# Attention and expert layers on one Trainium2 core: idle TensorE products moved to the first place, and the last part of q loaded by one DMA

## The chip, the cores and the metric

The kernel runs on one core of one Trainium2 chip. The metric is the device time of one execution in microseconds; several executions are made, and their median counts. A profiled execution of the kernel before gives the trace from which all rows below come.

## The reference

Two computations follow each other. The first is an attention with pooled queries, the second an expert layer over its output.

```python
q_pool = q.reshape(B, H, S // 2, 2, D).mean(axis=3)          # B 4, H 8, S 1152, D 64
scores = scale * np.matmul(q_pool, k.transpose(0, 1, 3, 2))
attn = exp(scores - max) / (sum + 1e-09)
x = np.matmul(attn, v)                                        # to 2304 tokens x 512
h = x @ w_in                                                  # 512 x 2048
g = np.where(h > 0.0, h, np.exp(np.minimum(h, 0.0)) - 1.0)
out = g @ w_out                                               # 2048 x 512
```

## The kernel before

The work of one batch item is a unit (four units); a unit has four pairs of heads, and a pair has nine attention steps: for each head four blocks of 128 pooled queries, and a last block of 64 for both heads together. A step computes scores on TensorE into the only score buffer `s` (L935 and L941 for a pair in plain float32, which the first pair is), takes their largest on VectorE into an `ep` buffer (`biggest`, L985), the exponential on ScalarE (L991), and turns the result by products with the identity (L1067) before it is multiplied with v. Since there is one buffer `s`, the scores of a step wait until L985 of the step before has read them. The expert layer of a unit (L1229, L1310) is spread between the attention steps of the next unit; the weights of both its matrices are first decoded on VectorE by three instructions each half (`dec`, L820, L821, L824), 512 KB a half.

Before the first step, `prep` fetches and turns the operands of the first pair. k comes in two DMAs on SP's queue (`load_k`, L600). q comes on ScalarE's queue: two DMAs of 256 KB, one for each head (`load_qa`, L585), and the last 128 rows of each head, 64 pooled queries, by `load_qb` (L591, with the issue at L593): a loop of two DMAs of 32 KB, each from 64 places of 512 bytes to 64 partitions. Behind them in SP's queue stand three halves of w_in (L805) and then the q of the second pair (L558, L563), which goes to the same tile and so waits until the first pair's q has been read. VectorE adds the two rows of each pooled query (`qtwice`, L655): blocks 4 to 7 first, then 0 to 3, then block 8, which is the part that `load_qb` brings. TensorE turns k and the sums (L624), ScalarE takes the results from PSUM (L627).

The order of the work on each engine is written out: `ORDER` (L32) lists task numbers with a letter for the engine (p TensorE, v VectorE, a ScalarE, g GpSimd, s the DMA queue of SP), and each engine works through its own tasks in exactly this order. `SLOTS` (L190) gives the buffer of each tile. In the list the addition of block 8 is `19v`; behind it on VectorE stand `301v` and `316v`, the decoding of the first two weight halves, and then `415v`, the first L985. ScalarE begins with `4a`, `3a` (load_qa) and `5a` (load_qb). TensorE begins with `11p` and `9p`, which turn k.

One task, `0p`, is `warm` (L758): six products of the identity with itself into a PSUM buffer that nobody reads. In the list before it stands between `20p`, the turning of block 8, and `437p`, the scores of the third step. The costs given to `plan.add` (900.0 for load_qb, 1530.0 for warm) belong to the planner that once wrote the list; the kernel as it is run reads the list only.

Of the kernel before, what the change touches and what calls it, by code (L numbers as in the profile page):

```python
# [19 lines left out]
CFG = dict(  # L20
    MODE=0,
    LOADS=-2465884, WI0=-27823, WIT=30440, WO0=1311932, WOT=4783, T0=1480, T1=812, M0=21242,
    M1=58392, KS=5164412, KM=-16195, KE=597808, KH=-20226, KL=126077, KV=-42119, KN=-15967,
    KX=-43605, KO=-36554, PEN=-18129, W0L=26355, WIN=-42633, PD=3605, KS0=29075649, KM0=3580,
    KE0=43169, KH0=-7128, KL0=17190, KV0=-37362, KX0=35076, PLM0=0, NS0=36, PLM=0, M2=6438, DP=0,
    FK=0, PENW=-13844, PENH=10146, FL=2000, PH0=2, PH=1, KT=140078, KT0=-327, LV=15492, PENN=-24464,
    PENT=-48259, PLP=1, WLP=1, HIP=1, PENM=0, L0=1000000, PA=9244, PB=93473, KA=40989, KB=-4257737, KC=34460,
    PENR=0,
# [1 line left out]


ORDER = """  # L32
2s 1s 11p 4a 16v 299s 9p 3a 314s 13v 5a 12a 10a 19v 17p 7p 283s 18a 414p 22s 288s 8a 301v 23s 316v
370s 294s 415v 14p 15a 427p 285v 20p 21a 428v 429a 0p 437p 435p 289s 431p 27p 34g 416a 31v 290v
319s 422p 438v 28a 404p 372v 32p 29p 439a 432a 423a 417g 405v 35p 25p 26a 406a 36a 291v 460p 461v
440g 441p 442a 321v 37g 42s 38p 40s 433p 30a 462a 434a 33a 450p 451v 443p 296v 418p 407g 436a 496p
497v 452a 419a 444a 293s 410p 420p 421a 45a 292a 39v 453g 458p 459v 408p 409a 6s 313s 309s 463v
# [150 lines left out]
"""  # L188

SLOTS = """  # L190
# [147 lines left out]
def attention_moe_kernel(  # L338
# [9 lines left out]
    nc = tc.nc  # L348
# [12 lines left out]
    plan = Plan()  # L361
# [40 lines left out]
    def act(n):  # L402
        return 0.95 * n + 70.0
# [4 lines left out]
    def dve(n):  # L408
        return Port(1.08 * n + 75.0)
# [4 lines left out]
    def pol(n):  # L414
        return 0.93 * n + 150.0

    def pol2(n):
        return Port(1.9 * n + 190.0)
# [18 lines left out]
    for b, s0, nt, lo in [(b, 0, 4, True) for b in range(0, B)]:  # L437
        u = Rec()
# [5 lines left out]
        while t0 < u.n:  # L444
            n = 256 if u.n - t0 != 320 else 320
# [102 lines left out]
    def prep(pr, t0, t1):  # L548
        u, p = pr.u, pr.p
        b, nq = u.b, u.nq  # L550
        q32, k32, qT, kT, v32 = (plan.buf(x) for x in ("q32", "k32", "qT", "kT", "v32"))
        pr.kT, pr.qT, pr.v32 = kT, qT, v32
        key = [t0 + (t1 - t0) * j / 16.0 for j in range(16)]
        lk = key[0] - (LOADS if pr.i else CFG["L0"])
# [27 lines left out]
        def load_qa(h):  # L582
            def load_qa():
                src, t = q[b, 2 * p + h, 2 * u.s0:], u.nt
                nc.scalar.dma_start(  # L585
                    out=q32.ap[:, t * h:t * h + t].rearrange("p t r d -> p (t r d)"),
                    in_=src[0:256 * t].rearrange("(p c) d -> p (c d)", p=128),
                )
            return load_qa

        def load_qb():  # L591
            for h in range(2):
                nc.scalar.dma_start(  # L593
                    out=q32.ap[64 * h:64 * h + 64, 2 * u.nt],
                    in_=q[b, 2 * p + h, 2 * u.s0 + 256 * u.nt:][0:128].rearrange("(p r) d -> p r d", r=2),
                )

        def load_k(h):
            def load_k():
                nc.sync.dma_start(out=k32.ap[:, h], in_=k[b, 2 * p + h].rearrange("(p c) d -> p c d", p=128))  # L600
            return load_k

        n = nq * 64
        q_s = lambda: q32.ap[:, :nq, 0]
        if pr.i == 0:
            tk = [plan.add("DMA", Move(450.0, 1100.0), lk + h, load_k(h), (), [k32], lag=LAND) for h in range(2)]
            tq = [plan.add("ACT", 450.0 + h, lk - 10.0 + h, load_qa(h), (), [q32]) for h in range(2)]
            tq.append(plan.add("ACT", 900.0, lk - 8.0, load_qb, (), [q32]))
        else:
            tq = [plan.add("DMA", Move(1700.0, 2200.0), lk - 10.0, load_q, (), [q32], lag=LAND)] * 3  # L610
        qa = None if pr.plain else plan.add("DVE", dve(n), key[0], qadd(nc.vector), [tq[0]], [q32], [("POOL", pol2(n) + 90.0, qadd(nc.gpsimd))])
# [62 lines left out]
        def hi(dst, src, j):  # L674
            def hi_act():
                nc.scalar.activation(out=dst(), in_=src(), func=AF.Copy, scale=sm.ap[:, 8 + j:9 + j])

            def hi_pool():
                ts(nc.gpsimd, dst(), src(), sm.ap[:, 8 + j:9 + j], 1.0)

            def hi_dve():
                ts(nc.vector, dst(), src(), sm.ap[:, 8 + j:9 + j], 1.0)

            hi_act.__name__ += str(j)
            return hi_act, hi_pool, hi_dve

        def lo(dst, src, h, j):
            def lo_dve():
                pairs_ = [(dst(), src(), h())]
                if len(dst().shape) == 4 and j <= 1:  # L690
                    pairs_ = [tuple(x()[:, :, a] for x in (dst, src, h)) for a in range(2)]
                for o, i, m in pairs_:
                    nc.vector.scalar_tensor_tensor(
                        out=o, in0=i, scalar=sm.ap[:, 8 + j:9 + j], in1=m, op0=ALU.mult, op1=ALU.subtract
                    )

            def lo_pool():
                ts(nc.gpsimd, src(), src(), sm.ap[:, 8 + j:9 + j], 1.0)
                nc.gpsimd.tensor_tensor(out=dst(), in0=src(), in1=h(), op=ALU.subtract)

            lo_dve.__name__ += str(j)
            return lo_dve, lo_pool

        def halves(n, kh, kl, dst_h, dst_l, src, j, after, bufs):
            f, g, d = hi(dst_h, src, j)
            h = plan.add("ACT", act(n), kh, f, after, bufs, [("POOL", pol(n), g), ("DVE", Port(0.58 * n + 90.0), d)])
            f, g = lo(dst_l, src, dst_h, j)
            t = plan.add("DVE", Port(730.0, 730.0) if j == 1 else dve(n) + 35.0 * (j == 0), kl, f, [h], bufs, [("POOL", Port(pol(n), pol2(n)), g)] if CFG["PLP"] else [])
            t.pen = CFG["PENH"]
            return t  # L710

# [19 lines left out]
        sc = summed(lambda: sm.ap[:, 0:nsum], nsum, key[3], sums, [sm], up)  # L731
        pr.sc = [sc]
        ql = halves(n, key[4], key[5], q_h, q_l, q_s, 0, [sc], [qn, q32, sm])

        def q_t():
# [14 lines left out]
        qw = plan.add("DMA", Move(1180.0, 1400.0), key[9], q_lo, [qt], [qT], lag=1000.0)  # L750
        pr.qs = lambda st: qw
        kl = halves(1152, key[6], key[7], k_h, k_l, k_s, 1, [sc, sums[-1]], [kn, k32, sm])
        pr.kdone = [[plan.add("DMA", Move(3400.0, 3000.0, True), key[9], k_t, [kl], [kn, kT], lag=1100.0)]] * 2
        pr.vdone = [halves(1152, key[11], key[12], v_h, v_l, v_s, 2, [sc], [v16, v32, sm])] if pr.split else [tv]

    idle = plan.buf("r")

    def warm():  # L758
        for i in range(6):
            nc.tensor.matmul(idle.ap[:, 0:128], ident, ident, start=True, stop=True)  # L760

    plan.add("PE", 1530.0, -1.0e9, warm, [], [idle])

    for pr in pairs:
        plan.at = str(pr.u.i)
        if pr.i == 0:
            prep(pr, -9000.0, 0.0)
        else:
            prev = pairs[pr.i - 1]
            prep(pr, prev.t0 - CFG["PA"], pr.t0 - CFG["PB"])  # L770
# [115 lines left out]
    r = plan.add("DVE", 150.0, WI0 + WIT * NG, wi_top, wi_max)  # L886
# [20 lines left out]
    r = plan.add("DVE", 150.0, 0.0, wo_top, wo_max)  # L907
# [476 lines left out]
```

## Time and profile before

| what | us |
| --- | --- |
| median of 3 executions | 742.1 (742.02 to 743.98) |
| profiled execution, its time | 742.65 |
| span of its trace, first to last instruction | 740.9 |
| TensorE busy in the span | 717.3 (97%) |
| VectorE busy | 625.0 (84%) |
| ScalarE busy | 560.6 (76%) |
| GpSimd busy | 338.0 (46%) |

The span is what the rows add up to; 1.75 us of the profiled execution lie outside it. Busy shares over the whole span hide that the engines take turns as the bound, so the rows below are of short stretches, most of them of the first 20 us, where the change is.

### The profile page before, as it was taken

Reading aid. Unit: us, or ns where it says so; the run is one execution under the profiler, and the core shown is the slowest. Engines: PE = TensorE matmul, PEld = TensorE weight load, DVE = VectorE, ACT = ScalarE, POOL = GpSimd, SP = SyncE. Lnnn points to the kernel's source line nnn. Section 1 sums busy time; section 2 is a strip of 40 time slices with the busy share of each in tenths; the row PEclk is TensorE's granted clock in tenths of the full one; section 3 lists DMA queues with packets and bytes.
Section 4 is the critical chain, followed back from the end, with each engine's and each line's share of the span. In section 5 each row is a group of like instructions: output and inputs, shape, how many; then the busy total and the mean of one; then the engine's idle time right before and its main releaser. Section 6 shows DMA issues by size and latency. Waiting matters only on the chain.

```text
span 740.9 us, 19632 instructions
## 1 busy us (share of the span) xinstructions
PE 717.3 (97%) x7905; PEld 478.8 (65%) x7905; DVE 625.0 (84%) x1098; ACT 560.6 (76%) x974; POOL 338.0 (46%) x385
## 2 busy tenths in 40 slices
PE   5899998999999999999999999999999999999997
PEld 4577776877565555775676566786665665865753
DVE  6999999999998998879898879899988989875330
ACT  3899997998998887777688766889788564752651
POOL 1322455466626633376465554354646452440430
PEclk9999999999999999999999999999999999999999
DMA  8787834577999998999999999899899998793001
GB/s 304 287 228 251 247 119 105 142 135 160 171 179 207 178 204 169 211 181 174 213 171 208 189 205 181 163 162 209 173 189 194 188 162 137 139 139 64 30 1 36
DMA packets 310971, 126.01 MB, mean 170 GB/s; under 512 B 286304, under 2 KB 288352, under 8 KB 310880
## 3 DMA queue, kind: packets, MB, share of 16 engines
q1 hardware_dynamic: 310432, 124.16, 82.4%
q8 instruction: 62, 1.02, 0.6%
q10 hardware_dynamic: 448, 0.59, 0.2%
q14 instruction: 29, 0.24, 0.1%
HBM read 45.09 MB, written 4.72 MB: 67 GB/s over the span
## 4 chain that ended last, share of the span: by engine, by line
PE 47%; DVE 3%; ACT 2%; issue 1%; DVEq 0%; ACTq 0%
PE r L1310 16%; PE r L1229 14%; PE r L1119 6%; PE s L956 4%; PE s L970 3%; PE r L1101 1%; DVE ep L985 1%; PE r L1067 1%; ACT ep L991 1%; PE s L961 0%; DVE ep L1045 0%; DVE tmp L1265 0%; DVE x L1207 0%; DVE g L1291 0%; ACT hb L1042 0%
## 5 line engine op out<-in xcount | busy, mean ns | idle before, releaser
L991 ACT ACTIVATE ep<-ep,wk 128x1152 f32<-128x1152 f32 x136 | 170.4, 1254 | 45.7 <-DVE ep L985 40.5
L1229 PE MATMUL r<-x,wi 128*128 128x256 f16 (+1 forms) x1536 | 196.6, 286 | 1.5 <-DVE tmp L1265 1.5
L985 DVE TENSOR_SCALAR_CACHE_REDUCE ep<-s,sm 128x1152 f32<-128x1152 f32 x122 | 172.3, 1412 | 13.0 <-PE s L970 9.2
L1229 PEld LDWEIGHTS <-wi 128*128 128x128 f16 x1536 | 147.6, 98 | 43.6 <-issue 6.1
L1310 PE MATMUL r<-wo,g 128*128 128x512 f16 (+1 forms) x864 | 174.9, 380 | 0.1
L1045 DVE SCALAR_TENSOR_TENSOR ep<-ep,wk,hb 128x1152 f16<-128x1152 f32 x99 | 146.0, 1478 | 6.7 <-ACT hb L1042 4.7
L1310 PEld LDWEIGHTS <-g 128*128 128x128 f16 (+1 forms) x864 | 73.3, 100 | 83.8 <-issue 4.7
L956 PE MATMUL s<-kT,qT 128*128 128x512 f16 (+3 forms) x420 | 82.9, 328 | 4.3 <-DVE ep L985 3.3
L1119 PEld LDWEIGHTS <-v 128*64 128x64 f16 x2970 | 77.8, 110 | 11.4 <-issue 10.5
L1119 PE MATMUL r<-pT,v 128*64 128x128 f16 (+1 forms) x2970 | 84.4, 215 | 0.3 <-DVE tmp L1265 0.3
L1283 POOL TENSOR_TENSOR g<-tmp,g 128x320 f16<-128x320 f32 (+1 forms) x61 | 68.1, 1118 | 36.0 <-ACT g L1279 34.4
L499 POOL TENSOR_SCALAR wk<-wk 128x1 f32<-128x1 f32 x68 | 31.2, 459 | 114.3 <-ACT ep L991 93.9
L1042 ACT ACTIVATE hb<-ep,wk 128x1152 f16<-128x1152 f32 x50 | 62.3, 1249 | 17.3 <-POOL wk L1010 8.2
L1036 POOL TENSOR_SCALAR hb<-ep,wk 128x1152 f16<-128x1152 f32 x34 | 44.3, 1303 | 56.6 <-DVE wk L1001 29.6
L1265 DVE SCALAR_TENSOR_TENSOR tmp<-r,tmp 128x320 f32<-128x320 f32 (+1 forms) x96 | 51.5, 551 | 21.5 <-POOL tmp L1250 11.5
L1242 ACT ACTIVATE tmp<-r 128x320 f32<-128x320 f32 (+1 forms) x96 | 45.1, 480 | 23.0 <-PE r L1229 14.7
L1245 ACT ACTIVATE tmp<-tmp,us 128x320 f32<-128x320 f32 (+1 forms) x96 | 57.8, 610 | 2.0 <-DVE us L1184 0.5
L956 PEld LDWEIGHTS <-qT 128*128 128x128 f16 (+1 forms) x420 | 33.9, 100 | 37.4 <-issue 13.7
L970 PE MATMUL s<-kT,qT 64*128 64x512 f16 (+1 forms) x280 | 49.6, 391 | 0.9 <-DVE ep L985 0.9
L1077 ACT ACTIVATE pT<-r 128x384 f32<-128x384 f32 x96 | 43.7, 498 | 8.7 <-PE r L1067 8.4
L1067 PE MATMUL r<-ident,ep 128*128 128x128 f32 x333 | 47.3, 283 | 2.3 <-DVE x L1134 2.3
L1287 POOL TENSOR_SCALAR g<-tmp 128x320 f16<-128x320 f32 (+1 forms) x42 | 28.8, 686 | 39.5 <-DVE tmp L1265 39.5
(163 smaller groups left out, 1044.0 us busy)
## 6 DMA issues: line engine op xcount, KB each, us to landing
v<-in_v_dram SPq DMA_DIRECT2D x16, 576.0 KB, 4.3
k<-in_k_dram SPq DMA_DIRECT2D x15, 576.0 KB, 4.5
g<-in_moe_w_in_dram SPq DMA_DIRECT2D x15, 512.0 KB, 7.2
q<-in_q_dram SPq DMA_DIRECT2D x15, 512.0 KB, 4.3
g<-in_moe_w_out_dram SPq DMA_DIRECT2D x15, 512.0 KB, 5.4
out_dram<-tmp SPq DMA_DIRECT2D x16, 256.0 KB, 3.0
qT<-qT SPq DMA_DIRECT2D x28, 144.0 KB, 3.0
pT<-hb SPq DMA_TRANSPOSE x99, 3.6
```

The source lines that it names most:

```text
L956: nc.tensor.matmul(s.ap[rows, c, 0:n], pr.qT.ap[:, 1 - c % 2, j, rows], keys[h][c], start=first[c], stop=not first[c] and c < 2, skip_grou ...
L970: nc.tensor.matmul(s.ap[rows, c, 0:512], pr.qT.ap[r, c, j, rows], keys[h][c][r], start=first[c], stop=not first[c], skip_group_check=True,)
L985: nc.vector.tensor_scalar(e_(), s.ap.rearrange("p a b -> p (a b)")[:, 0:S], -0.5 / float(D) ** 0.5 if pr.plain else pr.sm.ap[:, 12:13], No ...
L991: nc.scalar.activation(out=e_(), in_=e_(), func=AF.Exp, bias=nm.ap[:, 0:1], scale=-1.0, accum_out=nm.ap[:, 1:2],)
L1042: nc.scalar.activation(out=hb.ap, in_=e_(), func=AF.Copy, scale=nm.ap[:, 1:2])
L1045: nc.vector.scalar_tensor_tensor(out=e16(), in0=e_(), scalar=nm.ap[:, 1:2], in1=hb.ap, op0=ALU.mult, op1=ALU.subtract)
L1067: nc.tensor.transpose(tp.ap[:, c * 128:(c + 1) * 128], e_()[:, (j + c) * 128:(j + c + 1) * 128], ident)
L1119: nc.tensor.matmul(half(h), pr.v16.ap[:, h, order[c], e], p, start=(j + c == 0), stop=(j == 2 and c == NCH - 1), skip_group_check=True,)
L1229: nc.tensor.matmul(hp.ap[:, f * n:(f + 1) * n], w_in16[g][:, a, c, (f0 + f) * 128:(f0 + f + 1) * 128], x16.ap[:, e, c, g0:g0 + n], start=( ...
L1245: nc.scalar.activation(out=en.ap[:, :m], in_=en.ap[:, :m], func=AF.Exp, scale=us.ap[:, 8:9])
L1283: nc.gpsimd.tensor_tensor(out=l, in0=gv, in1=h, op=ALU.subtract)
L1310: nc.tensor.matmul(op.ap[r0:r0 + tn, :], gt[qd].ap[:, a, fi, o:o + tn], w_out16(f // 2)[:, e, f % 2, :], start=(i < 128 // tn), stop=(i >= ...
```

## The change

It makes three edits. The idle products are seven and stand first in TensorE's order. The last part of q comes by one DMA that covers both heads; its destination is 128 partitions of 512 bytes, its source two heads of 64 places of 512 bytes. Five PSUM buffers of the first part are renumbered: the idle products write buffer 0, and the turnings of k and q that used 3, 1, 2 and 0 use 4, 2, 3 and 1. The rest of `ORDER` and `SLOTS` is unchanged, and the changed costs are the planner's alone.

```diff
 ORDER = """
-2s 1s 11p 4a 16v 299s 9p 3a 314s 13v 5a 12a 10a 19v 17p 7p 283s 18a 414p 22s 288s 8a 301v 23s 316v
-370s 294s 415v 14p 15a 427p 285v 20p 21a 428v 429a 0p 437p 435p 289s 431p 27p 34g 416a 31v 290v
+0p 2s 1s 11p 4a 16v 299s 9p 3a 314s 13v 5a 12a 10a 19v 17p 7p 283s 18a 414p 22s 288s 8a 301v 23s
+316v 370s 294s 415v 14p 15a 427p 285v 20p 21a 428v 429a 437p 435p 289s 431p 27p 34g 416a 31v 290v
...
 SLOTS = """
-01 00 00 00 03 00 01 00 00 04 00 02 00 00 00 01 00 01 04 04 00 01 01 03 03 00 00 02 00 00 00 02 00
+00 00 00 00 04 00 02 01 00 00 00 03 01 00 00 01 00 01 04 04 00 01 01 03 03 00 00 02 00 00 00 02 00
...
         def load_qb():
-            for h in range(2):
-                nc.scalar.dma_start(
-                    out=q32.ap[64 * h:64 * h + 64, 2 * u.nt],
-                    in_=q[b, 2 * p + h, 2 * u.s0 + 256 * u.nt:][0:128].rearrange("(p r) d -> p r d", r=2),
-                )
+            nc.scalar.dma_start(
+                out=q32.ap[:, 2 * u.nt].rearrange("p r d -> p (r d)"),
+                in_=q[b, 2 * p:2 * p + 2, 2 * u.s0 + 256 * u.nt:][:, 0:128].rearrange("h (p r) d -> h p (r d)", r=2),
+            )
...
     def warm():
-        for i in range(6):
+        for i in range(7):
             nc.tensor.matmul(idle.ap[:, 0:128], ident, ident, start=True, stop=True)
 
-    plan.add("PE", 1530.0, -1.0e9, warm, [], [idle])
+    plan.add("PE", 1820.0, -1.0e9, warm, [], [idle])
```

## Rows read from the trace of the kernel before

**Rows 1.** Busy time by stretch: span, PE, PEld, DVE, ACT, POOL, PEclk, DMA, GB/s
```profile
core 0: us, PE busy (x) PEld busy (x) DVE busy (x) ACT busy (x) POOL busy (x), PEclk, DMA share, GB/s
...
6.00:9.00 3.00, 2.98 (x15) 2.67 (x15) 1.46 (x4) 1.47 (x3) 0.00 (x0) 1.00 1.06 384
9.00:12.00 3.00, 2.99 (x11) 1.55 (x10) 2.90 (x6) 0.60 (x1) 0.00 (x0) 1.00 0.94 269
12.00:15.00 3.00, 1.50 (x8) 0.97 (x9) 2.93 (x6) 0.60 (x1) 0.00 (x0) 1.00 0.89 280
...
60.00:90.00 30.00, 30.00 (x342) 23.18 (x342) 28.82 (x67) 28.73 (x59) 10.16 (x14) 1.00 0.86 263
...
117.00:124.00 7.00, 3.48 (x29) 2.35 (x24) 6.93 (x10) 5.18 (x11) 5.23 (x3) 0.99 0.71 190
124.00:127.30 3.30, 3.30 (x17) 2.41 (x14) 2.80 (x10) 0.58 (x2) 0.00 (x0) 0.51 0.89 187
...
300.00:600.00 300.00, 298.28 (x3529) 197.56 (x3528) 266.50 (x450) 231.83 (x394) 160.83 (x180) 1.00 1.00 188
```

**Rows 2.** Waits of VectorE, 8 to 124 us: total, times, longest
```profile
DVE kn L655 <- DMA q<-in_q_dram: 1.3, 1, 1.3
```

**Rows 3.** Timeline of VectorE, 4 to 20 us: start, duration, what, idle before
```profile
8.20 0.29 DVE L655 TENSOR_TENSOR kn<-q 128x128 f32<-128x128 f32 x1 [1.27 <-DMA q<-in_q_dram]
8.41 0.42 DVE L820 TENSOR_SCALAR tmp<-h 128x512 uint32<-128x512 uint32 x1
...
11.38 0.69 DVE L824 SCALAR_TENSOR_TENSOR wi<-g,tmp 128x512 uint32<-128x512 uint32 x1
11.99 1.35 DVE L985 TENSOR_SCALAR_CACHE_REDUCE ep<-s 128x1152 f32<-128x1152 f32 x1
...
15.06 1.35 DVE L985 TENSOR_SCALAR_CACHE_REDUCE ep<-s 128x1152 f32<-128x1152 f32 x1
```

**Rows 4.** Timeline of TensorE, 0 to 30 us
```profile
6.02 1.30 PE L624 MATMUL r<-ident,k 128*128 128x128 f32 x5 [6.02 <-DMA k<-in_k_dram]
...
8.96 2.08 PE L935 MATMUL s<-kT,qT 64*128 64x512 f32 x4
10.83 0.56 PE L941 MATMUL s<-kT,qT 64*128 64x128 f32 x2
11.33 0.66 PE L624 MATMUL r<-ident,kn 128*128 128x128 f32 x4
13.49 1.13 PE L935 MATMUL s<-kT,qT 64*128 64x512 f32 x4 [1.50 <-DVE ep L985]
14.43 0.38 PE L941 MATMUL s<-kT,qT 64*128 64x128 f32 x2
...
14.90 1.50 PE L760 MATMUL r<-ident 128*128 128x128 f32 x12
16.47 1.13 PE L935 MATMUL s<-kT,qT 64*128 64x512 f32 x4
```

**Rows 5.** Timeline of the first 30 us: GpSimd's last work on the identity, and load_qb's issues
```profile
1.00 0.29 POOL masks.py:199 TENSOR_SCALAR_AFFINE_SELECT ident<-ident 128x128 f32<-128x128 f32 x1
...
1.65 1.16 ACTq L593 DMA_DIRECT2D q<-in_q_dram  x2
```

**Rows 6.** DMA by queue, 0 to 30 us: packets, MB, share of 16 engines
```profile
q10 hardware_dynamic: 448, 0.59, 5.6%
```

**Rows 7.** DMA issues of 2.0 to 2.3 us: KB each, median us to landing
```profile
h<-in_moe_w_in_dram SPq DMA_DIRECT2D x1, 512.0 KB, 6.3
...
q<-in_q_dram ACTq DMA_DIRECT2D x2, 32.0 KB, 5.9
```

**Rows 8.** DMA issues of 1.6 to 1.7 us: the second load_qa
```profile
q<-in_q_dram ACTq DMA_DIRECT2D x1, 256.0 KB, 5.0
```

**Rows 9.** The third half of w_in: its issue in SP's timeline, 3.4 to 6 us
```profile
4.93 0.37 SPq L805 DMA_DIRECT2D g<-in_moe_w_in_dram  x1
```

**Rows 10.** DMA issues of 3.5 to 6 us: the same load's landing
```profile
g<-in_moe_w_in_dram SPq DMA_DIRECT2D x1, 512.0 KB, 5.6
```

More of the change, by code (lines that the diff above doesn't have):

```diff
@@ L607, in prep @@
             tq = [plan.add("ACT", 450.0 + h, lk - 10.0 + h, load_qa(h), (), [q32]) for h in range(2)]
-            tq.append(plan.add("ACT", 900.0, lk - 8.0, load_qb, (), [q32]))
+            tq.append(plan.add("ACT", 470.0, lk - 8.0, load_qb, (), [q32]))
         else:
@@ L707, in halves @@
             f, g = lo(dst_l, src, dst_h, j)
-            t = plan.add("DVE", Port(730.0, 730.0) if j == 1 else dve(n) + 35.0 * (j == 0), kl, f, [h], bufs, [("POOL", Port(pol(n), pol2(n)), g)] if CFG["PLP"] else [])
+            t = plan.add("DVE", Port(730.0, 730.0) if j == 1 else Port(*[0.5 * dve(n) + 17.5] * 2) if j == 0 else dve(n), kl, f, [h], bufs, [("POOL", Port(pol(n), pol2(n)), g)] if CFG["PLP"] else [])
             t.pen = CFG["PENH"]
```

## The prediction

> **What bounds the kernel now.** I read the busy time by stretch first, then who waits for whom, then the timeline of the first 20 us. In the middle, from 300 to 600 us, TensorE has no gaps worth the name: 298.28 of 300 us busy [rows 1]. But the change is made at the very start, and there another engine sets the pace. From 9 us on VectorE is busy 2.90 of every 3 us while TensorE drops to 1.50 [rows 1], and between 8 and 124 us VectorE waits for a measurable time exactly once: 1.3 us for a DMA of q [rows 2]. That wait ends at 8.20, when VectorE adds the last part of q [rows 3]; the last part is what the changed DMA brings. Behind it VectorE runs without a hole: two weight halves decoded from 8.41 to 12.07, the first L985 at 11.99, three more decoding instructions, the second L985 at 15.06 [rows 3]. At 117 to 124 us TensorE is the one that stands idle (3.48 of 7 us busy) beside a VectorE at 6.93 [rows 1]. So up to 124 us a delay of VectorE's chain at 8.20 is passed on whole, and after that TensorE's full queue passes it on too. Nothing downstream has slack to swallow it.
>
> The idle products stand at 14.90 to 16.40, and the next scores start at 16.47 [rows 4], when the second L985 has read the single buffer `s` (15.06 + 1.35 = 16.41 [rows 3]). They fill a hole; they hold up nothing.
>
> **The change, part by part.** *Six products taken from 14.9:* 12 instructions, 1.50 us [rows 4], worth nothing, since the cover is L985 and stays.
>
> *Seven put first:* they need only the identity, ready at 1.29 [rows 5]. Their price without warm-up is bounded by the same form later, 14 x 125 ns = 1.75 us, and by the slowest early turning, 1.30 us / 5 = 0.26 us each [rows 4], so 3.6 us. From 1.35 that ends at 3.1 to 5.0, ahead of 6.02, when k lands [rows 4]. Cost zero, with 1 us of cover left.
>
> What they could gain is a faster clock for TensorE's first real work. The clock column says 1.00 there, but the durations say otherwise: four score products take 2.08 us at 8.96 and 1.13 us at 13.49, and turnings go from 0.26 to 0.165 us at 11.33 [rows 4]. So up to about 11 us TensorE ran at the lower of its levels, 1.2 GHz, and then at 2.4. Yet a faster start pays almost nothing: the first scores end at 11.39 [rows 4], and L985 begins at 11.99 because VectorE is decoding until then [rows 3]. Between nothing and a few tenths; I take zero.
>
> *Buffers renumbered:* the turning that gets buffer 4 a second time stands behind the first scores in TensorE's order, and the buffer's reader is done by then. Zero.
>
> *The last part of q by one DMA.* On ScalarE's queue one issue goes (two take 1.16 us [rows 5]); ScalarE has nothing else to do then, so nothing. What counts is when the data land. Now the two DMAs start at 1.65 and 2.20 and land 5.9 us later [rows 5, 7], at 7.55 and 8.11, which is the 8.20 of VectorE.
>
> How is a DMA dealt out to the 16 engines? The queue of these four DMAs shows 448 packets [rows 6]. From the code, 256 are rows of 2 KB and 128 are places of 512 bytes; the 64 left are 16 for each DMA, one closing write per engine. So each ran on all 16. In each, both sides had 64 or 128 as their outermost length. In the new one the destination has 128, but the source has 2: the heads lie 1152 rows apart, so its two blocks cannot be read as one run. No row shows such a DMA. The ends are 16 engines and 2. Equal shares of the outermost length explain the 16 of all the old ones, and here leave only shares of two; I take 2 engines.
>
> The Trainium skill ("DMA: Bandwidth & Descriptors", section on why a DMA increments its semaphore by 16) gives this as the rule: the count is the largest up to 16 that divides the outermost lengths of both sides. By it the merged DMA runs on 2 engines, with 16 the sum would be about zero; no trace here has tested it yet.
>
> The price by rows: the 16 engines together move 384 GB/s between 6 and 9 us [rows 1], 24 GB/s each. Two engines get 32 KB each in place of 4 KB. At the least that is 28 KB more at 24 GB/s, 1.2 us: landing at 9.3. At the most, every 512-byte packet waits for a 2 KB packet of SP's queue: 64 times 2.5 KB at 24 GB/s is 6.8 us, from the landing of the second load_qa at 6.16 [rows 8] to 13.0. Between them: SP's early loads end with the third weight half, 4.93 + 5.6 = 10.5 [rows 9, 10], on these two engines 1.2 us later, 11.7; by then 52 of the 64 packets are through, and the rest take 0.3 us. I take 11.9, nearest to the upper end since the queues are full there: **3.8 us later** than 8.11.
>
> The weight half that is decoded next landed at 1.63 + 6.3 = 7.9 [rows 7], so it is not the next to be late. SP's queue is: the second pair's q waits for this tile, and all loads behind it with it; but their readers on VectorE move by the same 3.8 us.
>
> *What follows from the gap:* TensorE, done at 12.0, would wait until 13.49 + 3.8 = 17.3 for its second scores [rows 4], with one small turning in between. The one fall of the clock in these stretches came behind a hole: 3.48 of 7 us busy, then 0.51 granted [rows 1], so 1.2 GHz. Scores at half speed last 2.43 us (8.96 to 11.39) against 1.32 (13.49 to 14.81) [rows 4]: 1.1 us a step while the step is bound by this loop. I count one step, 1.1 us; none is the lower end, three (3.3 us) the upper.
>
> **The sum.** Profiled execution 742.65 + 3.8 + 1.1 = 747.5; the median lies 0.55 lower, so 742.1 + 4.9 = **747.0 us**. This case's own range: 742.1 + 1.2 = 743.3 to 742.1 + 4.9 + 3.3 = 750.3.
>
> **The rivals.** *Sixteen engines after all (not slower).* The merged DMA is one packet per engine shorter and lands between 7.55 and 8.11. VectorE then goes on until the weight half at 7.9 stops it, so it gains 0 to 0.3 us: 741.8 to 742.1. For it: every DMA in the trace used 16. Against: none had an outermost length of 2. It decides at the landing: below 8.2 it is this.
>
> *The hole at 14.9 costs the clock.* With the idle products gone and the DMA harmless, TensorE rests at 12.0 to 13.49 and again at 15.1 to 16.47. If the clock falls, one to three score steps cost 1.1 us each: 743.2 to 745.4. Against: 12 to 15 us has 1.50 of 3 us busy and the clock stays 1.00 [rows 1].
>
> *The early clock pays.* If the seven products raise the clock before 6 us and the DMA lands early, L985 starts 0.3 us sooner, 741.8, no more, by the decoding ahead of it.
>
> **How the numbers follow.** Two engines 0.60, sixteen with nothing else 0.30, the hole's clock alone 0.06, the early clock 0.04. A measurement tells 0.3%, 2.2 us: the limits are 739.9 and 744.3. Of the two-engine case about 0.08 stays under 744.3 (early landing, clock kept), 0.52 is above; of the hole 0.02 is above. That makes slower 0.54, and the rest, less 0.03 for what I have not seen, the same. The range runs from 741.0, below the sixteen-engine case by what executions scatter, to 749.3; it leaves the far end of the clock's fall out.
>
> **What would show it.** Right: block 8's addition at about 12 us, the first L985 at 15.8, slow score products near 17, and 384 + 16 + 16 + 2 = 418 packets on ScalarE's queue; 432 would mean sixteen engines. Wrong: that addition at 8.2 or sooner, with VectorE's chain where it was. If it comes at 12 and the end does not move, the claim that VectorE's chain is passed on whole was wrong.

## The result, and the profile after

The changed kernel takes 747.75 us (median of 6 executions, 745.76 to 749.44), the kernel before 742.06 us beside it: a ratio of 1.007 with a 95% interval of 1.0051 to 1.009, 5.7 us slower. The profiled execution took 749.06 us with a span of 747.3.

The first view is the timeline of VectorE in the changed kernel (start, duration, what, idle time before). Lines have moved up by one: L654 is the addition of q, L984 the first pass over the scores.

```profile
6.30 0.69 DVE L654 TENSOR_TENSOR kn<-q 128x512 f32<-128x512 f32 x1 [0.63 <-DMA q<-in_q_dram]
11.54 0.29 DVE L654 TENSOR_TENSOR kn<-q 128x128 f32<-128x128 f32 x1 [4.54 <-DMA q<-in_q_dram]
...
15.33 1.35 DVE L984 TENSOR_SCALAR_CACHE_REDUCE ep<-s 128x1152 f32<-128x1152 f32 x1
...
19.34 1.36 DVE L984 TENSOR_SCALAR_CACHE_REDUCE ep<-s 128x1152 f32<-128x1152 f32 x1 [0.86 <-PE s L940]
...
23.31 1.35 DVE L984 TENSOR_SCALAR_CACHE_REDUCE ep<-s 128x1152 f32<-128x1152 f32 x1
...
27.54 1.36 DVE L984 TENSOR_SCALAR_CACHE_REDUCE ep<-s 128x1152 f32<-128x1152 f32 x1 [1.08 <-PE s L940]
...
30.62 1.35 DVE L984 TENSOR_SCALAR_CACHE_REDUCE wo<-s 128x1152 f32<-128x1152 f32 x1
```

Block 8 is added at 11.54, where it was at 8.20 [rows 3]: VectorE stands idle for 4.54 us, waiting for the last part of q. The first L984 comes at 15.33 in place of 11.99 [rows 3], the same 3.34 us. Then a second loss joins: the next one is 4.28 us late (19.34 against 15.06 [rows 3]), and VectorE now waits for the scores, 0.86 and 1.08 us, which it never did before [rows 2]. The fifth starts at 30.62; in the kernel before it started at 24.86, so that 5.76 us are lost by then. This is the row of the kernel before, from the same view:

```profile
24.86 1.35 DVE L985 TENSOR_SCALAR_CACHE_REDUCE wo<-s 128x1152 f32<-128x1152 f32 x1
```

The second view is TensorE's timeline of the same stretch, the third the busy time by stretch with the granted clock (columns as in rows 1).

```profile
1.34 3.35 PE L759 MATMUL r<-ident 128*128 128x128 f32 x14 [1.34 <-POOL ident masks.py:199]
6.23 1.30 PE L623 MATMUL r<-ident,k 128*128 128x128 f32 x5 [1.53 <-DMA k<-in_k_dram]
...
9.15 1.13 PE L934 MATMUL s<-kT,qT 64*128 64x512 f32 x4
...
16.83 2.08 PE L934 MATMUL s<-kT,qT 64*128 64x512 f32 x4 [5.74 <-DVE ep L984]
...
20.76 2.08 PE L934 MATMUL s<-kT,qT 64*128 64x512 f32 x4 [1.05 <-DVE ep L984]
...
26.16 1.13 PE L934 MATMUL s<-kT,qT 64*128 64x512 f32 x4
```

```profile
9.00:12.00 3.00, 2.09 (x12) 1.10 (x10) 0.46 (x2) 1.21 (x3) 0.00 (x0) 1.00 0.19 65
12.00:16.00 4.00, 0.00 (x0) 0.00 (x0) 3.86 (x7) 0.00 (x0) 0.00 (x0) 0.99 0.59 185
16.00:19.00 3.00, 2.17 (x6) 1.19 (x6) 2.41 (x5) 0.00 (x0) 0.00 (x0) 0.50 1.01 379
19.00:24.00 5.00, 3.94 (x13) 2.17 (x13) 4.59 (x7) 2.87 (x5) 1.77 (x3) 0.50 0.97 369
24.00:30.00 6.00, 6.00 (x35) 4.42 (x34) 4.79 (x9) 3.48 (x7) 1.42 (x4) 0.82 0.03 13
...
125.00:132.00 7.00, 4.21 (x23) 2.54 (x22) 6.33 (x12) 3.15 (x8) 3.88 (x2) 0.75 0.76 202
```

The seven products run from 1.34 and are done at 4.7, before k lands. TensorE then has nothing at all to do between 12 and 16 us, and after that the granted clock is 0.50, which is 1.2 GHz, until the stretch 24 to 30, where it is back for most of the time. Two score steps fall into it: 2.08 us for products that take 1.13 at 9.15 and at 26.16. The clock falls once more near 125 us (0.75 over 125 to 132), as it did in the trace of the kernel before (0.51 over 124 to 127.3 [rows 1]).

The last view of the changed kernel is the DMA queue of ScalarE, 0 to 30 us (packets, MB, share of 16 engines).

```profile
q10 hardware_dynamic: 418, 0.59, 5.7%
```

It held 448 packets before [rows 6]; the prediction had put 418 for two engines and 432 for sixteen. The bytes are the same 0.59 MB.

### The profile page after: what moved, and what is told of

Read it like the earlier page. It is cut to its first block, busy times and chain, and to the rows that moved or that the text cites. A ratio compares the mean times of both kernels' runs of the same rounds, so it can differ in the third digit from the quotient of the medians.

```text
span 747.3 us, 19634 instructions
## 1 busy us (share of the span) xinstructions
PE 722.9 (97%) x7907; PEld 483.0 (65%) x7907; DVE 625.5 (84%) x1098; ACT 560.3 (75%) x974; POOL 339.8 (45%) x385
## 4 chain that ended last, share of the span: by engine, by line
PE 47%; DVE 4%; ACT 3%; issue 3%; POOL 2%; DVEq 0%; POOLq 0%; ACTq 0%
PE r L1309 16%; PE r L1228 14%; PE r L1118 6%; PE s L955 4%; PE s L969 3%; DVE ep L984 2%; PE r L1100 1%; ACT ep L990 1%; PE r L1066 1%; ACT hb L1041 1%; DVE tmp L1264 1%; POOL wk L1009 1%; PE s L960 0%; DVE ep L1044 0%; POOL wk L499 0%
## 5 line engine op out<-in xcount | busy, mean ns | idle before, releaser
L984 DVE TENSOR_SCALAR_CACHE_REDUCE ep<-s,sm 128x1152 f32<-128x1152 f32 x122 | 172.2, 1411 | 14.5 <-PE s L969 11.3
L1066 PE MATMUL r<-ident,ep 128*128 128x128 f32 x333 | 49.0, 290 | 2.3 <-DVE x L1133 2.3
```

The source lines that it names most:

```text
L984: nc.vector.tensor_scalar(e_(), s.ap.rearrange("p a b -> p (a b)")[:, 0:S], -0.5 / float(D) ** 0.5 if pr.plain else pr.sm.ap[:, 12:13], No ...
```

## The experiments

The theory: the merged DMA runs on two engines and is late, VectorE's chain hands this on whole, and the clock adds the rest. Against it stand the other edit, the moved idle products, and the merging as such.

**e1, the idle products moved, without the merged DMA.**

```diff
-            nc.scalar.dma_start(
-                out=q32.ap[:, 2 * u.nt].rearrange("p r d -> p (r d)"),
-                in_=q[b, 2 * p:2 * p + 2, 2 * u.s0 + 256 * u.nt:][:, 0:128].rearrange("h (p r) d -> h p (r d)", r=2),
-            )
+            for h in range(2):
+                nc.scalar.dma_start(
+                    out=q32.ap[64 * h:64 * h + 64, 2 * u.nt],
+                    in_=q[b, 2 * p + h, 2 * u.s0 + 256 * u.nt:][0:128].rearrange("(p r) d -> p r d", r=2),
+                )
```

> The changed kernel with load_qb back to two DMAs; the seven idle products stay in the first place. Theory (the merged DMA runs on two engines and lands 3.3 us late, and the hole behind it costs the clock): block 8 is added at 8.2, the first L985 is at 12.0, and the time is that of the kernel before, 741.5 to 742.5. Rival (the loss comes from the idle products that no longer stand at 14.9): the slow stretch of TensorE stays and the time is 744.5 to 748. Second rival (half and half): 744 to 745.

Measured: 744.96 us (12 executions, 741.88 to 746.79), ratio to before 1.0027 (1.0012 to 1.0043). The profiled execution has block 8 at 8.18, the first L985 at 11.97 and a span of 740.1: by its trace, the kernel before. But the executions differ. Their mean granted clock goes from 0.998 (741.91 us) to 0.988 (746.79 us), and most lie near 745 at 0.99. The time is the second rival's: with two DMAs, the kernel loses 2.46 us to the moved products. A single trace would have hidden it. Whether the two losses add up, e2 has to say.

**e2, the merged DMA without the moved products.** The kernel before with the new `load_qb`.

> The kernel before with load_qb as one DMA, and nothing else changed: six idle products between the second and the third scores. Theory: block 8 is added at 11.4 to 11.6, the first L985 is at 15.3, the second scores find a cold TensorE; the six products now stand behind them, up to 3 us at the lower clock, so the time is 746 to 750. Rival (the missing idle products are the cause): 742 to 743.5, since they are back.

Measured: 748.15 us (4 executions, 744.87 to 748.71), ratio 1.0067 (1.0043 to 1.0092). Block 8 is added at 11.62, the first pass is at 15.41, the second scores take 2.08 us from 16.92. The rival that puts all on the missing products falls. The merged DMA alone costs 5.65 us, as much as the whole change, so the losses of e1 and e2 do not add up: beside the merged DMA, the six products in their old place save nothing that four executions show. In the profiled execution, the fastest of the four, they do something all the same. TensorE's timeline:

```profile
16.92 2.08 PE L934 MATMUL s<-kT,qT 64*128 64x512 f32 x4 [5.33 <-DVE ep L984]
...
19.59 1.97 PE L759 MATMUL r<-ident 128*128 128x128 f32 x12
21.49 1.13 PE L934 MATMUL s<-kT,qT 64*128 64x512 f32 x4
```

Behind the six products the third scores are back at 1.13 us; without them, in the changed kernel, they take 2.08 from 20.76.

**e3, one DMA, but with an outermost length of 128.**

```diff
-                in_=q[b, 2 * p:2 * p + 2, 2 * u.s0 + 256 * u.nt:][:, 0:128].rearrange("h (p r) d -> h p (r d)", r=2),
+                in_=q[b, 2 * p, 2 * u.s0 + 256 * u.nt - 128:][0:256].rearrange("(p r) d -> p (r d)", r=2),
```

> The changed kernel with load_qb as one DMA of the same 64 KB to the same 128 partitions, but from 128 places in one row of the source (the last 256 rows of the first head), so that the source's outermost length is 128; the last queries of the second head are so replaced by others. Theory (it is the outermost length of 2, not the merging): ScalarE's queue shows 432 packets, block 8 is added at 7.9 to 8.3, and the time is 741.5 to 742.5. Rival (a DMA of 64 KB lands late because it is one, behind the queue): added at 10 us or later, 745 to 748, and 418 packets do not matter.

Measured: 744.94 us (10 executions, 742.21 to 746.24), ratio 1.0024 (1.0007 to 1.004). From the DMA queues (0 to 30 us) and the timelines of VectorE and TensorE of this kernel:

```profile
q10 hardware_dynamic: 432, 0.59, 5.7%
```

```profile
7.79 0.29 DVE L654 TENSOR_TENSOR kn<-q 128x128 f32<-128x128 f32 x1 [0.61 <-DMA q<-in_q_dram]
```

```profile
14.39 0.33 PE L623 MATMUL r<-ident,kn 128*128 128x128 f32 x1
16.12 2.08 PE L934 MATMUL s<-kT,qT 64*128 64x512 f32 x4 [1.40 <-DVE ep L984]
```

The same 64 KB in one DMA to the same partitions, 432 packets, and block 8 is added at 7.79, sooner than with two. So it is not the merging; what differs is the source, whose outermost length is 2 in one and 128 in the other. Lengths between were not tried, and the source of e3 is also one unbroken run, which that of the changed kernel is not. The time is not the 742 of the theory, but e1's: the slow third scores at 16.12 come behind the place where the six products had stood.

**e4, the long hole filled.** Sixteen idle products ahead of the turning of blocks 0 to 3, into its own PSUM buffer.

```diff
                 def flip_turn():
+                    for i in range(extra):
+                        nc.tensor.matmul(xp.ap[:, 0:128], ident, ident, start=True, stop=True)
                     for i, x in enumerate(blocks):
...
-                tq_.append(flip(blocks, lambda a=a, e=e: pr.q_f()[:, 128 * a:128 * e], key[8], [qa], qT, qq))
+                tq_.append(flip(blocks, lambda a=a, e=e: pr.q_f()[:, 128 * a:128 * e], key[8], [qa], qT, qq, 16 if pr.i == 0 and a == 0 else 0))
```

> The changed kernel with sixteen more idle products ahead of the turning of blocks 0 to 3, about 4 us of TensorE work in the hole before the second scores. Theory (3.3 us of the loss are the late landing, the other 2.4 us are the clock that fell in the hole): the second scores take 1.3 us in place of 2.5, the fifth L985 comes at 28.2 in place of 30.6, and the time is 745.0 to 746.0. Rival (the late landing accounts for all, the slow scores are hidden by VectorE): no change, 747.2 to 748.2.

Measured: 747.83 us (6 executions, 746.56 to 748.22), ratio 1.0067 (1.0051 to 1.0084). The profiled execution does what was expected of the stretch: the second scores take 1.13 us, and the fifth pass comes at 28.24.

```profile
16.87 1.13 PE L936 MATMUL s<-kT,qT 64*128 64x512 f32 x4 [1.68 <-DVE ep L986]
...
19.84 1.13 PE L936 MATMUL s<-kT,qT 64*128 64x512 f32 x4 [1.40 <-DVE ep L986]
```

The median does not move all the same. That execution (746.56 us) had a mean clock of 0.995, four of the six had 0.990. The hole ahead of the third scores, 1.40 us, is still open, and later ones too: in this trace the granted clock is 1.00 over 12 to 30 us and 0.58 over 125 to 132. One filled hole was not enough; where the clock fell in the four executions at 0.990 no trace shows. This expectation was wrong in its time.

**e5 and e6, the idle products by themselves.** e5 is the kernel before with seven more at the head of its first turning of k, so that both places are taken; e6 is the kernel before with none.

```diff
-            tk_.append(flip([kpair(4)], lambda: pr.k_f()[:, 1024:1152], key[9], [*dict.fromkeys(tk)], kT, k32))
+            tk_.append(flip([kpair(4)], lambda: pr.k_f()[:, 1024:1152], key[9], [*dict.fromkeys(tk)], kT, k32, 7 if pr.i == 0 else 0))
```

```diff
-        for i in range(6):
+        for i in range(0):
             nc.tensor.matmul(idle.ap[:, 0:128], ident, ident, start=True, stop=True)
```

> The kernel before (two DMAs, six idle products between the second and third scores) with seven more idle products in TensorE's first place. Theory (what the move of the idle products costs is the hole left at 14.9, where the clock falls in some executions): the time is that of the kernel before, 742.0 to 742.8, mean clock about 0.997. Rival (the early products shift or spoil the clock's rise): 744 to 746 as with the two DMAs alone, mean clock 0.99.

> The kernel before without any idle products. Theory (the hole at 14.9 is what costs): as with the two DMAs and the seven first, 744 to 746, mean clock 0.990 to 0.993. Rival (the early products are what costs): 742.0 to 742.8.

Measured: e5 742.03 us (12 executions, 740.2 to 743.73), ratio 0.9994 (0.9979 to 1.001); e6 745.42 us (12 executions, 742.36 to 748.0), ratio 1.0028 (1.0012 to 1.0045). With the six where they were, the seven neither help nor hurt; without any, the time is that of e1. So the seven in the first place are worth nothing that could be measured, and the six behind the second scores are worth 2.5 us (e1) to 3 us (e6, whose only edit they are: 745.42 against 742.46).

The profiled executions, one of each, show what they can do. In e6 the second and the third scores both take 2.08 us (13.66 and 17.59). In e5 the clock has fallen as well before the six products, and the second scores take 1.99 us (13.54); behind the six the third scores take 1.13 (18.00), as in e2. So the six do not only keep the clock up, they also go with its sooner return.

**e8, e1's kernel profiled once more.**

> The changed kernel with two DMAs for load_qb once more, for a second profiled execution. Theory: where its mean clock is 0.993 or less, the granted clock falls in the stretch 12 to 24 us, the third or fourth scores take 2.5 us in place of 1.3, and the span is 1.5 to 4 us over 740.1; where it is 0.997 or more, the span is 740 to 741. Rival: the clock falls elsewhere.

This execution took 745.25 us, span 743.4, mean clock 0.990. TensorE's timeline and the busy time by stretch:

```profile
10.46 0.66 PE L624 MATMUL r<-ident,kn 128*128 128x128 f32 x4
13.69 1.13 PE L935 MATMUL s<-kT,qT 64*128 64x512 f32 x4 [2.57 <-DVE ep L985]
...
16.66 2.08 PE L935 MATMUL s<-kT,qT 64*128 64x512 f32 x4 [1.40 <-DVE ep L985]
```

```profile
12.00:16.00 4.00, 1.57 (x7) 0.84 (x7) 3.93 (x7) 0.28 (x1) 0.65 (x1) 0.98 0.92 298
16.00:19.00 3.00, 2.34 (x6) 1.17 (x6) 2.93 (x6) 2.36 (x3) 0.61 (x1) 0.50 1.02 395
19.00:24.00 5.00, 5.00 (x23) 3.89 (x23) 3.36 (x7) 2.70 (x7) 1.22 (x4) 0.63 0.45 171
...
125.00:132.00 7.00, 6.28 (x29) 4.25 (x27) 5.68 (x17) 3.45 (x8) 0.13 (x1) 0.51 0.75 160
```

The clock falls behind the two holes, 2.57 and 1.40 us, and a second time behind the hole near 120 us, here for the whole stretch 125 to 132. The first profile of the same kernel has the holes too (1.52 and 1.40 us) and keeps the clock at 1.00 from 12 to 24 us. The two executions are not alike in their first hole, though: in e8 the first scores already run at the upper level (1.13 us from 9.18, in e1 1.98 from 9.16), so TensorE is done sooner and waits longer. Whether the longer hole decided or chance did, this pair does not tell. What does change from execution to execution of this one kernel is the mean clock, 0.988 to 0.998 in e1. The Trainium skill ("TensorE: Matmul & The Clock Gate", Part 1) says why this can be: the activity is looked at in a free-running rhythm that does not start with the kernel, so that the number of slow products varies between runs. The runs agree with the variation; the rhythm itself was not tested.

**e7, the holes filled in the kernel before.** Five idle products ahead of the second scores, and eight behind the last turning ahead of the hole at 120 us.

```diff
+            if t.n == 427:
+                warm_task = self.tasks[0]
+                for b in warm_task.bufs:
+                    if b.ap is None:
+                        b.ap = self.make[b.tag](b.slot)
+                self.idle_products(5)
             t.emit()
...
                     for c in range(3):
                         one(c)
+                    plan.turned += 1
+                    if plan.turned == 87:
+                        plan.idle_products(8, tp.ap[:, 384:512])
```

> The kernel before with five more idle products ahead of the second scores (the hole from 12.0 to 13.5) and eight in the hole from 120 to 122.3, both while TensorE waits. Theory (each of the kernel's falls of the clock costs about 1.7 us and comes behind one of these holes): mean clock 0.999 to 1.000 in nearly all executions, 740.3 to 741.2. Rival (the falls come from the total of the idle time around and are not to be filled this way, or the fillers delay the work behind them): 742.0 to 744.

Measured: **740.21 us** (11 executions, 740.11 to 740.63), ratio to before 0.9974 (0.9961 to 0.9987). It beats both kernels. Block 8 in VectorE's timeline, TensorE's timeline, and the span with the mean granted clock:

```profile
8.44 0.29 DVE L661 TENSOR_TENSOR kn<-q 128x128 f32<-128x128 f32 x1 [1.35 <-DMA q<-in_q_dram]
```

```profile
11.75 1.28 PE L772 MATMUL r<-ident 128*128 128x128 f32 x10
13.74 1.13 PE L948 MATMUL s<-kT,qT 64*128 64x512 f32 x4 [0.71 <-DVE ep L998]
...
15.15 1.50 PE L766 MATMUL r<-ident 128*128 128x128 f32 x12
16.72 1.13 PE L948 MATMUL s<-kT,qT 64*128 64x512 f32 x4
```

```profile
120.27 1.95 PE L772 MATMUL r<-ident 128*128 128x128 f32 x16
122.69 0.52 PE L1080 MATMUL r<-ident,ep 128*128 128x128 f32 x3 [0.47 <-DVE x L1150]
```

```profile
core 0: 738.7 us, clock 0.999
```

Every execution has 0.999 or 1.000, and the spread, 1.7 us and more in the kernels before it here, is 0.5 us. The kernel before does as well only when it keeps its clock (740.46 us the best of its 28 beside this one).

**e9, the merged DMA with the clock held.** e7 with the new `load_qb`, and twenty products in place of five for the longer hole.

> The version with both holes filled, but with load_qb as one DMA, and twenty idle products ahead of the second scores in place of five, for the longer hole; the clock should so be held at its upper level in both. Theory (the DMA costs its late landing, 3.2 to 3.5 us, and VectorE's chain hands it on whole; the rest of the loss was the clock): 743.3 to 743.9 beside 740.2, mean clock 0.999. Rival (part of the landing is swallowed later, and the clock was more of the loss): 741 to 742.5. Rival (fillers cannot hold the clock): 745 or more, mean clock 0.99.

Measured: 743.51 us (11 executions, 743.3 to 744.4), mean clock 0.999 or 1.000 in all. From the timelines of VectorE and TensorE, and the span:

```profile
11.51 0.29 DVE L660 TENSOR_TENSOR kn<-q 128x128 f32<-128x128 f32 x1 [4.37 <-DMA q<-in_q_dram]
```

```profile
11.83 4.63 PE L771 MATMUL r<-ident 128*128 128x128 f32 x40
16.80 1.13 PE L947 MATMUL s<-kT,qT 64*128 64x512 f32 x4 [0.34 <-DVE ep L997]
```

```profile
core 0: 741.7 us, clock 1.000
```

This is the landing alone, and it is handed on whole: in the two traces block 8 is added at 8.44 and 11.51 us, 3.07 apart, and the spans are 738.7 and 741.7 us, 3.0 apart. The medians are 743.51 - 740.21 = 3.3 us apart. e9 and e10 ran on another chip than e1 to e8, with the kernel before at 742.07 us (21 executions) beside them, not at 742.46 (28 executions) as beside e7. Each taken against the kernel before beside it, e9 and e7 are 3.7 us apart (1.44 above, 2.25 below).

What is left of the change's 5.7 us, some 2.4, is the clock, since little of it stays where the clock is held. How it is shared among the holes is not told apart. That e1 lost as much (2.46) does not make the moved products the cause: e2 has the six in place and loses 5.65. Filling the long hole alone (e4) or having the six back alone (e2) gained nothing in the median; both together with the later hole (e9) gained all of it.

**e10, the last part of q sooner.** e7 with `5a` ahead of `3a` in the list, so that load_qb's two DMAs go out before the second load_qa.

```diff
-2s 1s 11p 4a 16v 299s 9p 3a 314s 13v 5a 12a 10a 19v 17p 7p 283s 18a 414p 22s 288s 8a 301v 23s 316v
+2s 1s 11p 4a 16v 299s 9p 5a 3a 314s 13v 12a 10a 19v 17p 7p 283s 18a 414p 22s 288s 8a 301v 23s 316v
```

> The version with both holes filled and ScalarE's order of DMAs changed: load_qb's two go out before the second load_qa. Theory (VectorE's chain starts when the last part of q is there, and behind it waits for a weight half that lands at 7.9): block 8 is added at 7.2 to 7.6, the decoding starts at 8.0 to 8.2 in place of 8.4 to 8.6, and the time is 0.2 to 0.4 us less than 740.2. Rival (the second load_qa comes later by as much and holds VectorE in turn, or nothing that small is passed on): 740.1 to 740.4.

Measured: 742.59 us (11 executions, 741.73 to 743.39), 2.4 us above e7 and no better than the kernel before beside it (742.07; ratio 1.0003, 0.9994 to 1.0012). Neither the theory's gain nor the rival's 740.1 to 740.4 came. The second load_qa goes out 1.2 us later than it did (2.37 against 1.16 in e7) and is late by nearly 3, since it also takes longer to land (6.9 us against 5.2): VectorE gets to blocks 0 to 3 at 9.29, not 6.41, and block 8 follows there.

```profile
2.37 0.74 ACTq L591 DMA_DIRECT2D q<-in_q_dram  x1
```

```profile
9.29 0.89 DVE L661 TENSOR_TENSOR kn<-q 128x512 f32<-128x512 f32 x2 [3.61 <-DMA q<-in_q_dram]
```

The first pass over the scores is so 1.45 us late (13.68 against 12.23 in e7). The rest is the clock again: the five idle products no longer fill the hole ahead of the second scores, and the six behind them run for 2.77 us where they took 1.50.

```profile
15.19 1.13 PE L948 MATMUL s<-kT,qT 64*128 64x512 f32 x4 [3.08 <-DVE ep L998]
...
16.78 2.77 PE L766 MATMUL r<-ident 128*128 128x128 f32 x12
```

The four executions with a mean clock of 0.999 or 1.000 take 741.73 to 742.15 us, the seven at 0.996 to 0.998 take 742.36 to 743.39.

## Why the prediction was right, and where it was not

**The landing.** Right in its mechanism and nearly in its size. Forecast was a landing at 11.9, 3.8 us late; VectorE's wait ends at 11.54, 3.34 us late. That the source's shape decides, and not the merging, is shown by e3 beside the changed kernel: one DMA in both, 432 packets and 7.79 against 418 packets and 11.54. That it means two engines is read from the count: 418 is what two closing writes make. The rule of the Trainium skill ("DMA: Bandwidth & Descriptors", section on why a DMA increments its semaphore by 16) agrees with both counts of packets. The terms of the forecast itself (11.7 and 0.3) make 12.0 and not 11.9, which changes nothing.

**VectorE's chain.** Right. At a held clock, e9 beside e7, 3.07 us at block 8 become 3.0 us of span.

**The clock behind the gap.** Right in kind, too small: forecast was one slow score step, 1.1 us. The profiled execution has two, inside the range of none to three, and 5.76 - 3.34 = 2.4 us are lost by the fifth pass. That execution is one of the slower ones (749.06 us). The forecast of 747.0 was near 747.75 in part by luck: one term was 0.5 too large and the other 1.3 too small.

**"Worth nothing, since the cover is L985 and stays".** For the kernel with two DMAs this step failed. The six products at 14.9 held up nothing, as said, but the clock depends on them: without them and without the merged DMA the kernel takes 745 to 745.4 us (e1, e6), with them and the seven 742.03 (e5). In the sum for the merged DMA the zero did no harm, since there no price of them shows (747.75 without, 748.15 with them in e2); the forecast did not give that reason. The rival that said so (the hole at 14.9 costs the clock) got a chance of 0.06, because in the one trace of before the clock stayed at 1.00 over 12 to 15 us with 1.50 of 3 us busy [rows 1]. That row is of the kernel with the six in place and ends where they begin (14.90 [rows 4]), so it cannot show what the hole does that their removal opens. And one execution at 1.00 was no evidence that others keep it; e1 and e8 are one kernel with both outcomes.

**Sixteen engines, not slower, 741.8 to 742.1.** With the DMA made harmless this case comes out at 744.94 (e3), slower than before by an interval that leaves out no change. Its landing was as forecast (7.79), its time was not, for the reason just told. So the cases that end not slower got too large a chance. "Every DMA in the trace used 16" also went beyond [rows 6], which count the four of ScalarE's queue.

**The seven in the first place.** Right: done at 4.7, ahead of k, no cost and no gain (e5). In some executions the first scores then run at the upper level (1.13 us at 9.15 in the changed kernel, at 9.18 in e8), in others not (1.98 at 9.16 in e1); the first L985 waits for VectorE's decoding either way, as forecast.

**Buffers renumbered.** Zero, as far as is shown: e1 has the new numbers, and its profiled execution has block 8 and the first L985 where they were. There are seven new numbers and not five: two turnings go from 0 to 1, and that of blocks 0 to 3 goes from 4 to 0, the buffer of the idle products, which are done 5.7 us before it (4.7 and 10.43).

Not settled: which of e7's two fillers brings how much was not tried apart, nor how the change's 2.4 us of clock are shared among the holes. Nor was it tried whether fewer than six products at 14.9 would hold the clock.

## What to carry to other kernels

Before two DMAs are merged, look at the outermost length on both sides: here a length of 2 made the transfer land 3.3 us later, and the count of packets on the queue fitted two engines in place of sixteen. Work that fills a hole may hold up nothing and still be worth its place, since TensorE's clock can fall behind the hole; look for it in the mean granted clock and the spread of many executions, not in one trace. Effects on the clock do not add up from one edit to the next (e1, e2): only with the clock held (e7, e9) could the price of the DMA be read by itself. And an early wait of the engine that sets the pace is paid in full at the end, even where that engine is no longer the bound.

## What was not expected of the hardware

The merged DMA's issue occupied ScalarE's queue as long as the two together: 1.14 us against 1.16 [rows 5]. The one DMA of e3, with the same 64 KB, took 0.45.

```profile
1.65 1.14 ACTq L592 DMA_DIRECT2D q<-in_q_dram  x1
```

A few idle products at three places, 19 in all with the six that stood there, took the spread of a 740 us kernel from 740.46 to 744.68 (28 executions of the kernel before) down to 740.11 to 740.63, although they do no work. And 1.2 us of delay in the issue of one 256 KB load (e10) became nearly 3 us at its landing; the 16 engines were full then (a share of 1.05 over 6 to 9 us), but that this is the cause was not tried.
